# A gated linear attention and spatial-gating MLP on one core: issue order from a list scheduler in the source, grouped attention, a reciprocal for the second scan, and weight low halves on TensorE

## The chip, the cores and the metric

The kernel runs on one core of one Trainium2 chip. The metric is the device time of one execution in microseconds. The engines are TensorE (PE; its weight loads are shown as PEld), VectorE (DVE), ScalarE (ACT), GpSimd (POOL) and SyncE (SP), which here only issues DMAs. Each engine works through its instructions strictly in the order in which they were put into its queue and waits on semaphores for the others.

## The reference

Inputs are q, k, v and alpha of 4 batches, 8 heads, 768 positions and 48 elements a head, and the weights of an MLP (w_in 384 x 1024 and w_out 512 x 384 in float64, w_sg 768 x 768 in float32). First a recurrence over the positions, then the MLP on its result x:

```
state = alpha[:, :, t, :, None] * state + k[:, :, t] (outer) v[:, :, t]
y[:, :, t] = q[:, :, t] . state
x = y with the heads side by side                  # 4 x 768 x 384
h = gelu_tanh(x @ w_in);  u, v = halves of h       # 512 each
v_n = (v - mean) / sqrt(var + 1e-6) * g_ln         # over the 512
v_s = w_sg @ v_n + b_sg                            # over the 768 positions
out = x + (u * v_s) @ w_out
```

## The kernel before

**Attention in chunks.** The 768 positions of a batch are six chunks of 128; with four batches there are 24 chunks, numbered i. Heads lie in pairs: j counts four pairs, e the two heads of a pair, at partitions 0 and 64. For a chunk, `att_load` brings alpha (tile a) and k, q, v (tile kqv, two buffers). `att_prep` makes the running product of alpha from the chunk's start (pf, a scan with a floor) and its counterpart from the end (rf, a second scan backwards that starts from 1/pf at the chunk's end), multiplies q by pf and k by rf, stores pf's last column (pend) and tests alpha's range. `att_scores` multiplies k and q (sc), masks the product on VectorE (at, L176) and transposes k (tp, kn). `att_out` makes y from the state's block matrix s_bd (L211) and from at and v (L214) pair by pair, copies y into xf (two copies and six small DMAs, `pack_x`), and makes the state's update (dl, L223), which VectorE adds and decays (s_c) and ScalarE copies into s_bd.

**Precision.** The MLP's operands are split into a high and a low half of a faster 32-bit type, and each product is three matmuls (`mm3`, L243 to L245): high by high, high by low, low by high. `x_split` makes the halves of x (xh, xl). The weights are split when they come: `split_f32` for w_sg (twelve pieces), `split_f64` for w_in (eight pieces) and w_out (four), which build a float32 from the float64's two words on VectorE (L107, L109, L112, L116, L118) and the low half on GpSimd (L99, L119, L120).

**The MLP** has four products: V (`mlp_v`, one per chunk, 9 matmuls of 512 columns; then gelu, moments, the root on GpSimd, the norm and its halves), U (`mlp_u`, eight a batch, 9 matmuls of 384), P (`mlp_spatial`, mm_s, eight a batch, 18 matmuls; then scale on VectorE, the gate product on GpSimd, high half on ScalarE, low half on VectorE), and R (`mlp_out`, mm_o, six a batch, 12 matmuls; then x is added and the result stored). hf counts the two halves of the positions.

**Order.** The source runs the attention of batch b and, slab by slab between its chunks, P and R of batch b - 1; V and U of a batch follow behind its last chunk (batch 0 has them in between). FILL spreads the weight pieces over batch 0, WARM puts three matmuls without use before each of its y. The program is built with `schedule_with_timeline_sim=True`: a planner then reorders each engine's instructions by simulated times, so that scores and y of a chunk come to lie between single matmuls of the MLP. TensorE starts on twelve matmuls of 128x512 without use (wps).

Of the kernel before, what the change touches and what calls it, by code (L numbers as in the profile page):

```python
# [9 lines left out]
F32 = mybir.dt.float32  # L10
# [11 lines left out]
P = 128  # L22
# [13 lines left out]
WARM = (3, 3, 3, 3, 3, 3)  # L36
FILL = (0, 0, 2, 2, 2, 2, 2, 2, 2, 2, 2, 2, 4)
EPS = 1e-6
F64_MIN_AS_F32 = float(np.array(0x38100000, np.uint32).view(np.float32))


@with_exitstack
def tile_gla_gmlp(ctx: ExitStack, tc: tile.TileContext, aT, kqv, w_in, w_sgT, w_out, g_ln, b_sg, out):
# [4 lines left out]
    late = []  # L48
# [46 lines left out]
    def split_f32(dst_hi, dst_lo, src):  # L95
        raw = stage.tile([P, TH], F32, tag="raw32", name="raw32", bufs=2)
        nc.sync.dma_start(raw, src)
        nc.scalar.copy(dst_hi, raw)
        nc.gpsimd.tensor_tensor(dst_lo, raw, dst_hi.bitcast(F32), op=ALU.subtract)  # L99

    def split_f64(dst_hi, dst_lo, src):
        raw = stage.tile([P, TH, 2], I32, tag="raw64", name="raw64", bufs=3)
        nc.sync.dma_start(raw, src.bitcast(I32).rearrange("p (n two) -> p n two", two=2))
        w0, w1 = raw[:, :, 0], raw[:, :, 1]
        mag = stage.tile([P, TH], F32, tag="mag", name="mag", bufs=2)
        nc.scalar.activation(mag, w1.bitcast(F32), AF.Abs)
        nc.vector.tensor_scalar_max(mag, mag, F64_MIN_AS_F32)  # L107
        top = stage.tile([P, TH], I32, tag="top", name="top", bufs=2)
        nc.vector.tensor_scalar(  # L109
            top, mag.bitcast(I32), 3, 0x3FFFFFF8, op0=ALU.logical_shift_left, op1=ALU.bitwise_and,  # L110
        )
        nc.vector.scalar_tensor_tensor(top, w1, -0x40000000, top, op0=ALU.bitwise_and, op1=ALU.bitwise_or)  # L112
        topf = top.bitcast(F32)
        nc.scalar.copy(dst_hi, topf)
        pw = mag.bitcast(I32)
        nc.vector.tensor_scalar(pw, top, -0x800000, None, op0=ALU.bitwise_and)  # L116
        rest = pw.bitcast(F32)
        nc.vector.scalar_tensor_tensor(rest, w0.bitcast(U32), 2.0 ** -52, rest, op0=ALU.mult, op1=ALU.mult)  # L118
        nc.gpsimd.tensor_tensor(topf, topf, dst_hi.bitcast(F32), op=ALU.subtract)  # L119
        nc.gpsimd.tensor_tensor(dst_lo, topf, rest, op=ALU.add)  # L120

    def w_in_piece(half, j):
        sl = slice(j * TH, (j + 1) * TH)
        hi = wi_hi[:, half].rearrange("p k f -> p (k f)")[:, sl]
        lo = wi_lo[:, half].rearrange("p k f -> p (k f)")[:, sl]
        split_f64(hi, lo, w_in[half, :, sl])

    def w_sg_piece(s, j):
        sl = slice(j * TH, (j + 1) * TH)
        split_f32(ws_hi[:, s, sl], ws_lo[:, s, sl], w_sgT[s * P:(s + 1) * P, sl])  # L130
# [5 lines left out]
    st = {}  # L136

    def att_load(i):
        a = att.tile([P, NP * C1 + 1], F32, tag="a", name="a")
        nc.sync.dma_start(a, aT[i])  # L140
        kqv_t = att.tile([P, 3, NP, C], F32, tag="kqv", name="kqv_t")
        nc.sync.dma_start(kqv_t, kqv[i])
        st[i] = dict(a=a, k=kqv_t[:, 0], q=kqv_t[:, 1], v=kqv_t[:, 2])

    def att_prep(i):
        s = st[i]
        a, k, q = s["a"], s["k"], s["q"]
        n = NP * C1
        pf = att1.tile([P, NP, C1], F32, tag="pf", name="pf")
        nc.vector.tensor_tensor_scan(  # L150
            pf.rearrange("p j t -> p (j t)"), a[:, 0:n], p_flr.rearrange("p j t -> p (j t)"),
            initial=0.0, op0=ALU.mult, op1=ALU.max,
        )
        fl = r_flr[i % 2]
        nc.vector.reciprocal(fl[:, :, C], pf[:, :, C])
        rf = att1.tile([P, NP, C1], F32, tag="rf", name="rf")
        nc.vector.tensor_tensor_scan(  # L157
            rf.rearrange("p j t -> p (j t)")[:, ::-1], a[:, n:0:-1], fl.rearrange("p j t -> p (j t)")[:, ::-1],
            initial=0.0, op0=ALU.mult, op1=ALU.max,
        )  # L160
        nc.gpsimd.tensor_copy(pend[:, i], pf[:, :, C])
        nc.gpsimd.tensor_tensor(k, k, rf[:, :, 1:], op=ALU.mult)  # L162
        nc.vector.tensor_tensor(q, q, pf[:, :, 1:], op=ALU.mult)  # L163
        av = a[:, 0:n].rearrange("p (j t) -> p j t", t=C1)[:, :, 1:]
        nc.scalar.activation(av, av, AF.Relu, bias=alo, scale=-1.0, accum_out=low[:, i:i + 1])  # L165

    def att_scores(i):
        s = st[i]
        k, q = s["k"], s["q"]
        sc = ps.tile([P, 2, NP, C], F32, tag="sc", name="sc")  # L170
        for j in range(NP):
# [3 lines left out]
        at = att1.tile([P, 2, NP, C], F32, tag="at", name="at")  # L175
        nc.vector.tensor_tensor(  # L176
            at.rearrange("p e j t -> p (e j) t"), sc.rearrange("p e j t -> p (e j) t"),
            mask[:, None, :].to_broadcast([P, 2 * NP, C]), op=ALU.mult,
        )
        s["at"] = at  # L180
        if i % NCH < NCH - 1:
            tp = ps.tile([P, NP, P], F32, tag="tp", name="tp")
            for j in range(NP):
                nc.tensor.transpose(tp[:, j], k[:, j], ident)
            kn = att1.tile([P, NP, P], F32, tag="kn", name="kn")
            nc.scalar.copy(kn, tp)
            s["kn"] = kn

    def pack_x(xf, tsl, y):
        y3 = att.tile([P, C], F32, tag="y3", name="y3")  # L190
        nc.scalar.copy(y3, y[:, NP - 1])
        nc.scalar.copy(xf[:, :, tsl], y[:, 0:NK])
        for kk in range(NK):
            for e in range(2):
                nc.sync.dma_start(
                    xf[64 * e + D:64 * e + 64, kk, tsl], y3[64 * e + 16 * kk:64 * e + 16 * kk + 16, :],
                )

    def keep_warm(o, n):
        for _ in range(n):  # L200
            nc.tensor.matmul(o.rearrange("p j t -> p (j t)"), warm[:, :P], warm, start=True, stop=True)

    def att_out(i, xf):
        b, c = divmod(i, NCH)
        s = st[i]
        y = ps.tile([P, NP, C], F32, tag="y", name="y")
        if b == 0:
            keep_warm(y, WARM[c])
        for j in range(NP):
            if c > 0:  # L210
                nc.tensor.matmul(y[:, j], s_bd[:, j], s["q"][:, j], start=True, stop=False)  # L211
            for e in range(2):
                r = slice(64 * e, 64 * e + 64)
                nc.tensor.matmul(y[r, j], s["v"][:, j, r], s["at"][:, e, j], start=(c == 0), stop=True)  # L214
        tsl = slice((c % CPH) * C, (c % CPH + 1) * C)
        pack_x(xf, tsl, y)
        if c < NCH - 1:
            dl = ps.tile([P, NP, D], F32, tag="dl", name="dl")
            kn = s["kn"]
            for j in range(NP):  # L220
                for e in range(2):
                    r = slice(64 * e, 64 * e + 64)
                    nc.tensor.matmul(dl[r, j], kn[:, j, r], s["v"][:, j, 64 * e:64 * e + D], start=True, stop=True)  # L223
            pb = pend[:, i, :, None].to_broadcast([P, NP, D])
            if c > 0:
                nc.vector.tensor_tensor(s_c, s_c, dl, op=ALU.add)
                nc.vector.tensor_tensor(s_c, s_c, pb, op=ALU.mult)
            else:
                nc.vector.tensor_tensor(s_c, dl, pb, op=ALU.mult)
# [289 lines left out]
```

## Time and profile before

| | us |
|---|---|
| median of three runs (lowest, highest) | 445.02 (444.12, 446.96) |
| span of the profiled execution, first to last instruction | 439.6 |
| median less span | 5.4 |
| PE busy, PEld busy | 402.6, 336.9 |
| DVE, ACT, POOL busy | 279.7, 147.0, 174.5 |

The profile is of one execution. "Busy" is the time in which an engine had an instruction in work; matmuls overlap, and their durations run over the next one's start, so the distance from start to start tells the price of one. A row of the timeline gives start, duration, engine, line, operation, tiles and count, and in brackets how long the engine had stood idle and what ended that. A group's row gives the sum of busy time and the mean of one in ns. A row of a stretch gives, after its length, the busy time and count of PE, PEld, DVE, ACT and POOL, the granted TensorE clock (1.00 is full), the DMA engines' share and GB/s.

### The profile page before, as it was taken

The numbers are of one execution on the slowest core, as the hardware profiler recorded it, in microseconds if no ns is written. First come the engines' busy times: TensorE is split into PE (matmuls) and PEld (weight loads), VectorE is DVE, ScalarE is ACT, GpSimd is POOL, SyncE is SP. The second block draws the span as 40 slices with busy tenths as digits, with TensorE's granted clock in tenths as the row PEclk, the third lists the DMA queues.
The fourth block names the chain that finished last, engine by engine and source line by source line (L and its number), as shares of the span: only waits on it lengthen the run. The fifth ranks groups of instructions, "written<-read, shape, count | busy, mean of one in ns | idle before, by whom it ended". The sixth has DMA issues, their size and how long they took to land.

```text
span 439.6 us, 7271 instructions
## 1 busy us (share of the span) xinstructions
PE 402.6 (92%) x2724; PEld 336.9 (77%) x2728; DVE 279.7 (64%) x410; ACT 147.0 (33%) x330; POOL 174.5 (40%) x200
## 2 busy tenths in 40 slices
PE   6489586978899999999999999999999999999994
PEld 2356375657788878788988887788988887899993
DVE  8999999999544676565454656665465732732331
ACT  2533553643332332254232331353222321541010
POOL 3756687787240432423230632423232530412030
PEclk9959788999999999999999999999999999999999
DMA  8744643451024332302024332202123201000101
GB/s 309 240 136 137 207 148 97 156 171 29 26 78 136 118 102 60 122 5 74 24 78 137 119 102 93 88 5 73 26 76 131 78 5 38 22 2 0 53 2 60
DMA packets 18762, 39.15 MB, mean 89 GB/s; under 512 B 4000, under 2 KB 10912, under 8 KB 18720
## 3 DMA queue, kind: packets, MB, share of 16 engines
q1 hardware_dynamic: 18720, 38.61, 26.8%
q8 instruction: 23, 0.38, 0.3%
q14 instruction: 19, 0.16, 0.1%
HBM read 32.70 MB, written 4.72 MB: 85 GB/s over the span
## 4 chain that ended last, share of the span: by engine, by line
PE 56%; DVE 16%; DMA 7%; issue 2%; ACT 1%; SPq 1%; POOL 1%; DVEq 0%; POOLq 0%
DMA kqv_t<-in_kqv 6%; PE mm_s L243 6%; PE mm_s L245 5%; PE mm_s L244 5%; DVE pf L150 4%; PE y L214 4%; PE y L211 4%; PE mm_u L243 3%; PE mm_v L243 3%; PE sc L174 3%; PE mm_o L244 3%; PE mm_v L244 3%; PE mm_u L245 3%; PE mm_u L244 3%; PE mm_v L245 3%; PE mm_o L243 3%
## 5 line engine op out<-in xcount | busy, mean ns | idle before, releaser
L283 POOL TENSOR_TENSOR g<-g,u 128x384 f32<-128x384 f32 x32 | 32.4, 1014 | 100.3 <-DVE g L282 100.2
L243 PE MATMUL mm_s<-ws_hi,vh 128*128 128x384 f32 x192 | 67.6, 352 | 0.0
L245 PE MATMUL mm_s<-ws_hi,vl 128*128 128x384 f32 x192 | 64.8, 339 | 2.2 <-DVE vl L265 2.2
L244 PE MATMUL mm_s<-ws_lo,vh 128*128 128x384 f32 x192 | 64.8, 338 | 0.0
L162 POOL TENSOR_TENSOR kqv_t<-kqv_t,rf 128x512 f32<-128x512 f32 x24 | 36.9, 1537 | 63.0 <-DMA kqv_t<-in_kqv 56.1
L214 PE MATMUL y<-at,kqv_t 128*64 128x128 f32 x384 | 42.9, 307 | 12.2 <-DVE at L176 12.0
L211 PE MATMUL y<-kqv_t,s_bd 128*128 128x128 f32 x160 | 39.0, 328 | 3.5 <-ACT s_bd L232 2.7
L150 DVE TENSOR_TENSOR_SCAN pf<-a,p_flr 128x516 f32<-128x516 f32 x24 | 41.1, 1713 | 1.3 <-DMA a<-in_aT 0.7
L284 ACT CAST gh<-g 128x384 fp32r<-128x384 f32 x32 | 16.5, 514 | 74.1 <-POOL g L283 74.1
L285 DVE TENSOR_TENSOR gl<-g,gh 128x384 fp32r<-128x384 f32 x32 | 19.2, 600 | 32.8 <-ACT gh L284 32.7
L214 PEld LDWEIGHTS y<-at,kqv_t 128*64 128x64 f32 x384 | 21.1, 142 | 23.7 <-DVE at L176 14.4
L211 PEld LDWEIGHTS y<-kqv_t,s_bd 128*128 128x128 f32 x160 | 26.9, 200 | 15.6 <-issue 10.6
L282 DVE SCALAR_TENSOR_TENSOR g<-mm_s,g_col,b_bc 128x384 f32<-128x384 f32 x32 | 19.6, 613 | 29.7 <-PE mm_s L245 29.7
L165 ACT ACTIVATE a<-a,alo 128x512 f32<-128x512 f32 x24 | 17.4, 723 | 62.9 <-DVE rf L157 62.8
L245 PEld LDWEIGHTS mm_s<-ws_hi,vl 128*128 128x128 f32 x192 | 36.1, 188 | 2.5 <-DVE vl L265 2.5
L243 PEld LDWEIGHTS mm_s<-ws_hi,vh 128*128 128x128 f32 x192 | 36.1, 188 | 1.2 <-DVE r L292 0.3
L243 PE MATMUL mm_u<-xh,wi_hi 128*128 128x384 f32 x96 | 35.1, 369 | 2.1 <-ACT vg L253 2.1
L163 DVE TENSOR_TENSOR kqv_t<-kqv_t,pf 128x512 f32<-128x512 f32 x24 | 18.9, 789 | 27.4 <-DMA kqv_t<-in_kqv 27.4
L244 PEld LDWEIGHTS mm_s<-ws_lo,vh 128*128 128x128 f32 x192 | 36.2, 188 | 0.0
L174 PEld LDWEIGHTS sc<-kqv_t 64*128 64x128 f32 x384 | 26.6, 191 | 10.7 <-issue 9.4
L174 PE MATMUL sc<-kqv_t 64*128 64x128 f32 x384 | 34.3, 295 | 0.0
L244 PE MATMUL mm_o<-gl,wo_hi 128*128 128x384 f32 x96 | 33.6, 350 | 0.5 <-DVE gl L285 0.2
(86 smaller groups left out, 870.1 us busy)
## 6 DMA issues: line engine op xcount, KB each, us to landing
kqv_t<-in_kqv SPq DMA_DIRECT2D x24, 768.0 KB, 4.3
a<-in_aT SPq DMA_DIRECT2D x24, 258.5 KB, 2.7
out_x<-r SPq DMA_DIRECT2D x24, 192.0 KB, 2.3
raw<-in_w_in SPq DMA_DIRECT2D x8, 384.0 KB, 4.1
raw<-in_w_sgT SPq DMA_DIRECT2D x12, 192.0 KB, 3.2
xf<-y SPq DMA_DIRECT2D x144, 8.0 KB, 2.6
raw<-in_w_out SPq DMA_DIRECT2D x4, 384.0 KB, 3.2
b_bc<-in_b_sg SPq DMA_DIRECT2D x1, 384.0 KB, 7.7
```

The lines of the kernel that those rows point to most:

```text
L150: nc.vector.tensor_tensor_scan(pf.rearrange("p j t -> p (j t)"), a[:, 0:n], p_flr.rearrange("p j t -> p (j t)"), initial=0.0, op0=ALU.mult ...
L162: nc.gpsimd.tensor_tensor(k, k, rf[:, :, 1:], op=ALU.mult)
L163: nc.vector.tensor_tensor(q, q, pf[:, :, 1:], op=ALU.mult)
L174: nc.tensor.matmul(sc[:, e, j], k[r, j], q[r, j], start=True, stop=True)
L211: nc.tensor.matmul(y[:, j], s_bd[:, j], s["q"][:, j], start=True, stop=False)
L214: nc.tensor.matmul(y[r, j], s["v"][:, j, r], s["at"][:, e, j], start=(c == 0), stop=True)
L243: nc.tensor.matmul(o, lh, rh, start=(idx == 0), stop=False)
L244: nc.tensor.matmul(o, lh, rl, start=False, stop=False)
L245: nc.tensor.matmul(o, ll, rh, start=False, stop=(idx == n - 1))
L282: nc.vector.scalar_tensor_tensor(g, o, g_col[:, d:d + 1], b_bc[:, tsl], op0=ALU.mult, op1=ALU.add)
L283: nc.gpsimd.tensor_tensor(g, g, u, op=ALU.mult)
L285: nc.vector.tensor_tensor(gl[:, d], g, gh[:, d].bitcast(F32), op=ALU.subtract)
```

## The change

- Every piece of work becomes a step with an engine, a cost in ns, the steps it follows and the buffers it takes. `Plan.issue` walks through them once, in Python, and emits each step's instructions in the order of a list scheduler: of the steps that could start soonest on an engine, the one that is due first. A list of TensorE's products, `units`, written by hand, gives the dues. The built-in planner is off inside (`manual_schedule`). Some steps (k, x low, gate, the low halves not on TensorE) go to GpSimd or VectorE, the norm to VectorE or ScalarE, whichever would end first by the plan.
- Attention comes in groups: the outputs of chunk i - 1 (O) and the scores of chunk i (S) one behind the other, with whole products of the MLP between the groups.
- The second scan, its floor r_flr and the small reciprocal go. After q is multiplied by pf, pf is inverted in place (128x512) and k multiplied by it. kqv has three buffers.
- The state stays in s_c; its block matrix s_bd and the copies into it go. The state's product is eight 64x64 matmuls ahead of all of at and v, not one 128x128 for each pair between them.
- The low halves of w_in and of w_sg's first half are made on TensorE (identity times the value less identity times the high half, in PSUM) and copied by ScalarE. w_sg's first half comes in two loads through the tiles gh and gl. w_out and w_sg's second half get their place from the plan. The raw tiles share one ring of two.
- WARM and FILL go; the first warm-up matmuls are 128x128. mask and p_flr become bf16.

The core of the diff:

```
+    REACH = {"pe": 215, "act": 40, "dve": 40, "pool": 75, "sp": 0}
...
+    def issue(self, units, ahead):
...
+            for e, c in ready.items():
+                t0 = min(x[0] for x in c)
+                t, way_order, n, way = min((x for x in c if x[0] <= t0 + (150 if e == "pe" else 60)), key=lambda x: x[1])
+                if best is None or (t, way_order) < best[:2]:
+                    best = (t, way_order, n, way)
...
-        nc.vector.reciprocal(fl[:, :, C], pf[:, :, C])
-        rf = att1.tile([P, NP, C1], F32, tag="rf", name="rf")
-        nc.vector.tensor_tensor_scan(
-            rf.rearrange("p j t -> p (j t)")[:, ::-1], a[:, n:0:-1], fl.rearrange("p j t -> p (j t)")[:, ::-1],
...
+    def invert(i):
+        pf = st[i]["pf"][:, :, 1:]
+        nc.vector.reciprocal(pf, pf)
...
-            if c > 0:
-                nc.tensor.matmul(y[:, j], s_bd[:, j], s["q"][:, j], start=True, stop=False)
...
+        if c > 0:
             for j in range(NP):
                 for e in range(2):
                     r = slice(64 * e, 64 * e + 64)
+                    nc.tensor.matmul(
+                        y[r, j], s_c[r, j], s["q"][r, j], start=(j == 0), stop=False, skip_group_check=True,
+                    )
...
+        def low_pe():
+            t["o"] = o = psm.tile([P, TH], F32, tag="mm", name="mm_w")
+            nc.tensor.matmul(o, ident, t["top"].bitcast(F32), start=True, stop=False)
+            nc.tensor.matmul(o, nident, dst_hi, start=False, stop=False)
+            nc.tensor.matmul(o, ident, t["mag"], start=False, stop=True)
...
+        plan.add(("recip", i), "dve", 670, lambda i=i: invert(i), [("q", i), ("pend", i)])
+        plan.add(
+            ("k", i), "pool", 1250, lambda i=i: scale_k(i, nc.gpsimd), [("recip", i), ("kqv", i)],
+            other=("dve*", 670, lambda i=i: scale_k(i, nc.vector)),
+        )
...
+    def group(i):
+        r = [(("O", i - 1), 2400)]
+        if i < n:
+            r.append((("S", i), 1500))
+        return r
...
+        for d in range(ND):
+            units.append((("P", b, 0, d), 3120))
+            if d > 0:
+                units.append((("U", b, 1, d), 1560))
+        if b < B - 1:
+            units += group(g + 2)
+            units += [(("R", b, 0, kk), 2080) for kk in range(NK)] + [(("P", b, 1, 0), 3120)]
+            units += group(g + 3)
+            units += [(("P", b, 1, d), 3120) for d in (1, 2, 3)]
+            units += group(g + 4)
...
+    keep_warm(ps.tile([P, NP, C], F32, tag="y", name="wps"), NWARM)
+    with tc.manual_schedule():
+        plan.issue([name for name, _ in units], 4)
```

By `units`, batch 0 runs O and S of its six chunks with V0 to V3 strewn in, then U of its first half, V4, V5, the scores of chunk 6 and one U, the group of O6 and S7, and then its first P. In later batches V3, the four U of the first half, V4, V5, one U and a group stand ahead of the first P.

More of the change, by code (lines that the diff above doesn't have):

```diff
@@ L42, in tile_gla_gmlp, with run @@
+def run(steps):
+    for s in steps:
+        (s[0] if isinstance(s[0], tuple) else s)[2]()
 @with_exitstack
@@ L47, in tile_gla_gmlp @@
     mlp = ctx.enter_context(tc.tile_pool(name="mlp", bufs=1))
-    late = []
     dram = ctx.enter_context(tc.tile_pool(name="dram", bufs=1, space=bass.MemoryType.DRAM))
@@ new lines, in split_f32, with load, high, low_half @@
+    def split_f32(dst_hi, dst_lo, src, raw=None):
+        t = dict(raw=raw)
+        def load():
+            raw = stage.tile([P, TH, 2], I32, tag="raw", name="raw", bufs=2)
+            t["raw"] = raw.bitcast(F32).rearrange("p n two -> p (n two)")[:, 0:TH]
+            nc.sync.dma_start(t["raw"], src)
+        def high():
+            nc.scalar.copy(dst_hi, t["raw"])
+        def low_half(eng):
+            eng.tensor_tensor(dst_lo, t["raw"], dst_hi.bitcast(F32), op=ALU.subtract)
+        def low_pe():
+            t["o"] = o = psm.tile([P, TH], F32, tag="mm", name="mm_w")
+            nc.tensor.matmul(o, ident, t["raw"], start=True, stop=False)
+            nc.tensor.matmul(o, nident, dst_hi, start=False, stop=True)
+        def low_act():
+            nc.scalar.copy(dst_lo, t["o"])
+        return dict(load=load, high=high, low_half=low_half, low_pe=low_pe, low_act=low_act, parts=t)
@@ L222, in att_out @@
                     r = slice(64 * e, 64 * e + 64)
[L223 to L229, printed above, removed]
+                    nc.tensor.matmul(
+                        y[r, j], s_c[r, j], s["q"][r, j], start=(j == 0), stop=False, skip_group_check=True,
+                    )
@@ L277, in mlp_spatial @@
+    def mlp_spatial(vn, u, g, hf, d):
         sl = slice(d * P, (d + 1) * P)
         tsl = slice(hf * TH, (hf + 1) * TH)
-        o = psm.tile([P, TH], F32, tag="mm", name="mm_s")
-        mm3(o, [(vn[s][0][:, sl], vn[s][1][:, sl], ws_hi[:, s, tsl], ws_lo[:, s, tsl]) for s in range(NS)])
-        g = late[0].tile([P, TH], F32, tag="g", name="g", bufs=2)
-        nc.vector.scalar_tensor_tensor(g, o, g_col[:, d:d + 1], b_bc[:, tsl], op0=ALU.mult, op1=ALU.add)
-        nc.gpsimd.tensor_tensor(g, g, u, op=ALU.mult)
@@ L284, in mlp_spatial @@
[L284 to L294 removed]
+        t = {}
@@ new lines, in product, with scale, gate @@
+        def product():
+            t["o"] = psm.tile([P, TH], F32, tag="mm", name="mm_s")
+            mm3(t["o"], [(v["vh"][:, sl], v["vl"][:, sl], ws_hi[:, s, tsl], ws_lo[:, s, tsl]) for s, v in enumerate(vn)])
+        def scale():
+            t["g"] = mlp.tile([P, TH], F32, tag="g", name="g", bufs=2)
+            nc.vector.scalar_tensor_tensor(
+                t["g"], t["o"], g_col[:, d:d + 1], b_bc[:, tsl], op0=ALU.mult, op1=ALU.add,
+            )
+        def gate(eng):
+            eng.tensor_tensor(t["g"], t["g"], u["u"], op=ALU.mult)
@@ new lines, in high, with low_half @@
+        def high():
+            if d == 0:
+                g["h"] = mlp.tile([P, ND, TH], F32R, tag="gh", name="gh")
+            nc.scalar.copy(g["h"][:, d], t["g"])
+        def low_half():
+            if d == 0:
+                g["l"] = mlp.tile([P, ND, TH], F32R, tag="gl", name="gl")
+            nc.vector.tensor_tensor(g["l"][:, d], t["g"], g["h"][:, d].bitcast(F32), op=ALU.subtract)
+        return [
+            ("pe", 3120, product), ("dve", 585, scale),
+            (("pool", 1000, lambda: gate(nc.gpsimd)), ("dve*", 545, lambda: gate(nc.vector))), ("act", 510, high),
+            ("dve*", 545, low_half),
+        ]
@@ new lines, in count @@
+    def count():
+        check["cnt"] = cnt = ps.tile([1, 1], F32, tag="dl", name="cnt")
+        nc.tensor.matmul(cnt, okp, ones, start=True, stop=True)
+    end = due[("R", B - 1, 0, 0)]
+    plan.add(("ok",), "dve", 600, in_range, [("range", n - 1), ("pend", n - 1)], due=end)
+    plan.add(("cnt",), "pe", 100, count, [("ok",)], takes=[("dl", 1, [("cnt_i",)])], due=end + 3000)
+    plan.add(("cnt_i",), "dve", 150, lambda: nc.vector.tensor_copy(cnt_i, check["cnt"]), [("cnt",)], due=end + 6000)
```

752 lines of the change are left out of this document (518 added, 234 removed).

## Prediction

> **What bounds the kernel now.** I read the busy totals and the tenths first, then the span cut where its character changes, then each engine's instructions in order of time.
>
> ```profile
> PE 402.6 (92%) x2724; PEld 336.9 (77%) x2728; DVE 279.7 (64%) x410; ACT 147.0 (33%) x330; POOL 174.5 (40%) x200
> DVE  8999999999544676565454656665465732732331
> ...
> 0.00:106.40 106.40, 80.40 (x548) 56.85 (x552) 102.85 (x139) 48.05 (x111) 73.03 (x82) 0.89 0.50 166
> 106.40:433.00 326.60, 322.13 (x2178) 280.08 (x2176) 176.01 (x271) 98.95 (x220) 101.46 (x119) 1.00 0.20 64
> 433.00:439.60 6.60, 0.05 (x1) 0.00 (x0) 0.88 (x2) 0.00 (x0) 0.00 (x0) 0.88 0.29 97
> ...
> 20.00:40.00 20.00, 15.52 (x102) 9.92 (x103) 19.97 (x25) 7.26 (x18) 14.62 (x13) 0.74 0.43 135
> ```
>
> Two kernels run one after the other. Up to 106.4 us, where the first mm_s product starts, VectorE is busy 102.85 us: it sets the pace, and the DMA engines are half idle. From 106.4 to 433.0 TensorE is busy 322.13 of 326.60 and VectorE only 176. Then comes a tail of 6.6. The 92% of the first line is a mean over both. So work taken from VectorE counts only in the first stretch, work taken from TensorE only in the second. The span is 439.6; the median of the three runs is 445.02, so 5.4 us lie around it, which I carry over.
>
> What fills VectorE up to 111 us, group by group (busy sum, mean):
>
> ```profile
> L150 DVE TENSOR_TENSOR_SCAN pf<-a,p_flr 128x516 f32<-128x516 f32 x10 | 14.5, 1447 | 0.8 <-DMA a<-in_aT 0.7
> L118 DVE SCALAR_TENSOR_TENSOR mag<-raw,mag 128x384 f32<-128x384 uint32 x12 | 14.3, 1195 | 0.0
> L157 DVE TENSOR_TENSOR_SCAN rf<-a,r_flr 128x516 f32<-128x516 f32 x10 | 13.7, 1375 | 0.2
> L112 DVE SCALAR_TENSOR_TENSOR top<-raw,top 128x384 int32<-128x384 int32 x12 | 11.4, 952 | 0.1
> L107 DVE TENSOR_SCALAR mag<-mag 128x384 f32<-128x384 f32 x12 | 9.1, 755 | 0.8 <-ACT mag L106 0.7
> L109 DVE TENSOR_SCALAR top<-mag 128x384 int32<-128x384 int32 x12 | 6.2, 521 | 0.1
> L116 DVE TENSOR_SCALAR mag<-top 128x384 int32<-128x384 int32 x12 | 4.8, 402 | 0.1
> ...
> 28.49 0.53 DVE L112 SCALAR_TENSOR_TENSOR top<-raw,top 128x384 int32<-128x384 int32 x1
> ...
> 29.05 0.36 DVE L116 TENSOR_SCALAR mag<-top 128x384 int32<-128x384 int32 x1
> 29.33 0.35 DVE L107 TENSOR_SCALAR mag<-mag 128x384 f32<-128x384 f32 x1
> ...
> L118 DVE SCALAR_TENSOR_TENSOR mag<-raw,mag x12: 559/1291/1373, 15.7 to 97.5; 128x384 f32<-128x384 uint32 x12
> ```
>
> The five steps of the twelve float64 pieces sum to 45.8 us, 3.8 a piece. The single rows show what they take undisturbed: 0.53, 0.36, 0.35, and 0.56 as L118's shortest, some 2.1 a piece with L109 like L107. The rest goes while GpSimd runs its own products beside them (73 us busy in this stretch).
>
> **The change, part by part.**
>
> *Second scan to reciprocal.* Ten second scans in the stretch, 13.7 us, go; a reciprocal of 128x512 comes, which the trace has only with four elements.
>
> ```profile
> L155 DVE RECIPROCAL r_flr<-pf x24: 157/169/183, 4.9 to 340.5; 128x4 f32<-128x4 f32 x24
> ...
> L438 DVE TENSOR_REDUCE ok_range<-pend 128x1 f32<-128x96 f32 x1 | 0.3, 253 | 0.0
> ...
> L437 DVE TENSOR_REDUCE ok_range<-low 128x1 f32<-128x24 f32 x1 | 0.2, 177 | 0.1
> ```
>
> Two reduces give 76 ns for 72 elements, so 1.06 ns an element over 152 ns. Four elements at that pace make 156, and 186 at eight times it; the reciprocal shows 157 to 183, median 169, nearer the first. Bounds: 0.69 and 4.5 us; I take 0.69. The Trainium skill (VectorE: DVE Perf Modes, "First, the fixed hardware budget") says that reciprocal is an iterative divide with a repeat count of 8; read as eight passes an element it speaks against this edit, at 4.5. No run here shows a long one; it is a rival below.
>
> *Weights.* The four w_out pieces go behind the first spatial products: 4 x 3.8 = 15.3 us leave the first stretch. The low halves of the eight w_in pieces go from GpSimd to TensorE and ScalarE, so their VectorE steps should run near 2.1 instead of 3.8: 13.6 us. VectorE's first stretch becomes 102.85 - 13.7 - 15.3 - 13.6 + 8 x 0.69 = 66; two chunks fewer are prepared ahead (two scans, 2.9): 63, and less if the other operations are disturbed less. It runs from about 3.6 on, so its work ends near 67; were GpSimd to disturb the pieces as now, near 80. The loads move too: w_sg's first halves come as two transfers instead of six, the raw ring shrinks from three and two buffers to two; the DMA share is 0.50 now, and the same bytes or fewer are wanted before the first P, so I cost that at nothing, hidden behind the work of VectorE and TensorE; uncovered it is the landing of one transfer at a time. ScalarE gets fourteen low halves and loses the copies into the state's block matrix; with 48 us busy of 106 it hides either, and the state comes to the next y without that copy. Steps for which either GpSimd or VectorE is picked (k, x low, gate) change sides at like cost, since the one disturbs the other; I count them as they are now.
>
> *TensorE's own prices,* as start-to-start distances:
>
> ```profile
> 8.07 1.16 PE L174 MATMUL sc<-kqv_t 64*128 64x128 f32 x16
> ...
> 139.00 1.16 PE L174 MATMUL sc<-kqv_t 64*128 64x128 f32 x16
> 140.10 0.66 PE L184 MATMUL tp<-ident,kqv_t 128*128 128x128 f32 x4
> 140.51 0.42 PE L243 MATMUL mm_s<-ws_hi,vh 128*128 128x384 f32 x1
> ...
> 146.24 0.44 PE L214 MATMUL y<-at,kqv_t 128*64 128x128 f32 x4
> 146.61 0.49 PE L211 MATMUL y<-kqv_t,s_bd 128*128 128x128 f32 x2
> 147.03 0.44 PE L214 MATMUL y<-at,kqv_t 128*64 128x128 f32 x4
> 147.30 0.62 PE L223 MATMUL dl<-kqv_t,kn 128*64 128x48 f32 x14
> 147.85 0.44 PE L243 MATMUL mm_s<-ws_hi,vh 128*128 128x384 f32 x1
> ...
> 166.29 0.38 PE L211 MATMUL y<-kqv_t,s_bd 128*128 128x128 f32 x2
> 166.43 0.42 PE L243 MATMUL mm_o<-gh,wo_hi 128*128 128x384 f32 x1
> ...
> 189.63 1.09 PE L214 MATMUL y<-at,kqv_t 128*64 128x128 f32 x16
> 190.65 0.49 PE L174 MATMUL sc<-kqv_t 64*128 64x128 f32 x2
> ...
> 386.26 0.40 PE L243 MATMUL mm_v<-wi_hi,xh 128*128 128x512 f32 x1
> 388.36 0.34 PE L243 MATMUL mm_u<-xh,wi_hi 128*128 128x384 f32 x1
> ...
> 394.72 0.34 PE L243 MATMUL mm_s<-ws_hi,vh 128*128 128x384 f32 x1
> 397.90 0.34 PE L243 MATMUL mm_s<-ws_hi,vh 128*128 128x384 f32 x1
> ```
>
> V (9 matmuls) is 2.10, P (18) is 3.18, so U (9) is 1.59 and R (12) 2.12; 63.4 a batch. Scores 1.10, transposes 0.41, dl 0.63 (14 in 0.55). A y with state is four times L211 and L214, 0.42 + 0.37: 3.16. But sixteen L214 in one go take 1.02, so 2.14 belongs to the state product and to changing shape eight times. Afterwards the state product is sixteen 64x64 instructions in one block. Bounds: the same pace as L214 (1.02) and no two beside each other (16 x 0.107 = 1.7, from the pair's 0.21 below). I take 1.05, nearest in shape: a y costs 2.07, **1.09 less in each of 20 chunks**.
>
> A low half on TensorE is two or one float32 products of 384 columns and a short one. The L211 pair inside the mm_o stream costs 0.14 and a slow step behind it, about 0.21 for 128 columns: 0.64 for 384 (bounds 0.4, three times L214's pace, and 1.26, three times 0.42). A w_in piece is 2 x 0.64 + 0.17 = 1.45, a w_sg piece 0.81: 16.5 in all, every bit in the first stretch.
>
> *TensorE's first stretch afterwards.* Seven scores 7.7, six transposes 2.5, six y 6.1 + 5 x 1.05, five dl 3.2, V 12.6, U of one half 6.4, low halves 16.5, changes of shape 1.3: 61.5. From 8.1 (first scores; the reciprocal path scan, q, reciprocal, k is no longer than now) that is **69.6 at the least**, a little behind VectorE. Both feed each other: scores, mask and outputs of a chunk follow one another, and the six mask products of 1.2 us have only weights and V to cover them. I add 8.4 and take **78** for the start of the first P (70 to 92).
>
> *The second stretch.* Now it holds, by the counts of its rows, P and R of batch 0 (38.1), three batches (190.2), 14.75 y with state (46.6), 2.25 without (2.3), 16.5 scores (18.2), 14 transposes (5.7), 14 dl (8.8): 309.9. The other 16.7 of 326.6 are 4.5 idle and 12.2 of changing shape, since scores and y are strewn in between the MLP's matmuls. Afterwards: 38.1 + 190.2, four U left over (6.4), 18 y 18.4 and their 15 state products 15.8, 15 dl 9.5, 17 scores 18.7, 14 transposes 5.7: 302.7. O and S come as a group, so I leave 8 for idling and shape (3 to 20): **311**.
>
> *Waits that are added.* An S stands right behind O; what waits on it in TensorE's queue is all the MLP work behind, and for that ScalarE and VectorE. A third kqv buffer starts its load two groups ahead, which covers the k product. VectorE and GpSimd have 150 us of room each in 311. V5's matmuls wait for six pack transfers on SP's queue, x high and low; V3, four U and V4 (10.5 us) cover that.
>
> *Tail.* R's products are no longer mixed by depth, so the last R waits at its tenth matmul for the last gate:
>
> ```profile
> 426.83 0.62 DVE L282 SCALAR_TENSOR_TENSOR g<-mm_s,g_col,b_bc 128x384 f32<-128x384 f32 x1 [0.27 <-PE mm_s L245]
> ...
> 429.19 0.56 DVE L285 TENSOR_TENSOR gl<-g,gh 128x384 fp32r<-128x384 f32 x1 [1.74 <-ACT gh L284]
> ```
>
> From scale to low half 2.9, and 0.3 before; nine matmuls cover 1.6: 1.6 more (0 to 3).
>
> **Sum:** 78 + 311 + 6.6 + 1.6 = 397; with 5.4 around it **402 us**. Against now: first stretch -28, second -16, tail +1.6.
>
> **Rivals.**
> *A slow start.* Eighteen keep-warm matmuls go and the first twelve shrink to a quarter.
>
> ```profile
> 22.97 0.69 PE L214 MATMUL y<-at,kqv_t 128*64 128x128 f32 x4 [4.48 <-DVE at L176]
> ```
>
> After this wait four L214 take 0.62 where they take 0.37 elsewhere, and the granted clock of 20 to 40 us is 0.74. At 0.74 throughout, 61.5 become 83: P starts at 91, with the same mask waits partly inside, so 415, to 425 if they are not. For it: the waits are where the recurrence is serial. Against: 61 us of work in 70 leave fewer long gaps than 80 busy in 106. The Trainium skill (TensorE: Matmul & The Clock Gate, "HAM oscillation — how this bites in real kernels") says that a gap beyond about 3.4 us halves the clock; by that rule, too, gaps and not sums decide, and the 4.48 above agrees.
> *A long reciprocal.* At 4.5 us VectorE gets 8 x 3.8 = 30 more in the first stretch: P at 100 to 108, and 425 to 433 in all, more with the later 16. The four-element row speaks against it.
> *Groups that stall, slower than now.* The order is fixed by constants; the second stretch's scans run beside GpSimd. If k comes late at each group, TensorE stands still, and nothing of the MLP may pass. There are 18 groups; 43 us are to be lost, so it decides from 2.4 us a group and is slower by 1% from 2.7: 450 to 460 at 3. Against: 4.5 us idle in all of that stretch now.
> *The list order is no better than the planner's.* Then the weights disturb as before: VectorE's first stretch is 102.85 - 13.7 + 5.5 and its start of 3.6, so 98, and the second stretch keeps all 16.7 of idling and shape, 319: 98 + 319 + 8.2 + 5.4 = 431, and up to 445 where w_out's work, no longer early, is late instead. For it: both orders are made from costs, not from the chip. Against: what costs most, w_out's steps and the low halves, is moved by the dependences and the engine, not by the order.
>
> **Chances.** Forecast (387 to 412) 0.68; slow start (412 to 428) 0.15; long reciprocal 0.05; stalled groups 0.07; no better order 0.05. Range **387 to 428**, leaving out most of the last three, 0.17. Three runs tell about 1% from no change. Slower is the stalled groups, 0.07; within 1% I put 0.04, the upper ends of the long reciprocal and of no better order; faster 0.89.
>
> **What would show it.** P's first matmul near 78 and VectorE near 0.9 busy before; reciprocals of 0.69; the pieces' last VectorE step (rest) near 0.56; sixteen 64x64 instructions in about 1.05; second stretch near 311 with TensorE at 0.97; granted clock near 0.9 at the start; the last R waiting about 1.6 us once. Wrong: a first P past 92, or waits of TensorE on k or q summing to over 10 us.

## The result, and the profile after

The changed kernel takes **430.2 us** (426.3 to 431.1), the kernel before in the same runs 444.6: a ratio of 0.966, with an interval from 0.960 to 0.973. It is faster, by 14 us and not by the 43 of the forecast; 402 was said, and 430 lies 2 us past the upper end of the range. Medians and ratios, here and below, leave out a few executions in a slower state, two of them of 1.2 and 2.1 ms.

First the busy totals and VectorE's tenths of the kernel after, then its span cut at the first P and at the last product (stretch, busy time and count of PE, PEld, DVE, ACT and POOL, granted clock, DMA share, GB/s).

```profile
PE 385.2 (90%) x2928; PEld 342.3 (80%) x2928; DVE 321.1 (75%) x466; ACT 145.2 (34%) x337; POOL 39.3 (9%) x87
...
DVE  6889999798996799797948778975848675353341
```
```profile
0.00:110.26 110.26, 80.44 (x613) 61.91 (x614) 98.82 (x144) 51.60 (x123) 11.64 (x31) 0.88 0.45 155
110.26:422.60 312.34, 304.77 (x2318) 280.39 (x2316) 221.91 (x323) 93.57 (x215) 27.62 (x56) 0.99 0.21 70
422.60:428.30 5.70, 0.00 (x0) 0.00 (x0) 0.39 (x1) 0.00 (x0) 0.00 (x0) 0.74 0.13 43
```

The first P starts at 110.3, 3.9 later than before, where 78 was forecast. Ahead of it VectorE is busy for 98.8 us (102.9 of 106.4 before), where 63 was forecast. The second stretch is 312.3 (326.6 before, 311 forecast). The profile of the kernel before is one of its shortest executions (a span of 439.6, where its other runs reach 446.2), so differences of a few us to its stretches are not exact. And work has changed sides: VectorE went from 279.7 to 321.1 in all, GpSimd from 174.5 to 39.3. VectorE's groups show what it is busy with:

```profile
L337 DVE RECIPROCAL pf<-pf 128x512 f32<-128x512 f32 x24 | 80.3, 3344 | 2.0 <-ACT pend L329 1.4 <-ACT u L520 0.5
L323 DVE TENSOR_TENSOR_SCAN pf<-a,p_flr 128x516 f32<-128x516 f32 x24 | 29.4, 1224 | 2.0 <-DMA a<-in_aT 1.9
...
L540 DVE TENSOR_TENSOR g<-g,u 128x384 f32<-128x384 f32 x32 | 17.8, 556 | 0.8
...
L341 DVE TENSOR_TENSOR kqv_t<-kqv_t,pf 128x512 f32<-128x512 f32 x23 | 15.7, 681 | 0.2
...
L439 DVE TENSOR_TENSOR xl<-xf,xh 128x384 fp32r<-128x384 f32 x23 | 12.3, 536 | 7.9 <-ACT xh L435 7.9
```

The reciprocal takes **3.34 us**, not 0.69. That is 80.3 us in all, 63.7 more than forecast and more than twice what the scan that it replaced takes (1.38 before, by L157). The last three rows are steps for which the plan may pick an engine: all 32 gate products, 23 of 24 k and 23 of 24 x low went to VectorE, on which the reciprocal already lies.

### The profile page after: what moved, and what is told of

Read it like the earlier page. It is cut to its first block, busy times and chain, and to the rows that moved or that the text cites. A ratio compares the mean times of both kernels' runs of the same rounds, so it can differ in the third digit from the quotient of the medians.

```text
span 428.3 us, 7480 instructions
## 1 busy us (share of the span) xinstructions
PE 385.2 (90%) x2928; PEld 342.3 (80%) x2928; DVE 321.1 (75%) x466; ACT 145.2 (34%) x337; POOL 39.3 (9%) x87
## 4 chain that ended last, share of the span: by engine, by line
PE 62%; DVE 17%; issue 6%; DMA 4%; ACT 4%; SPq 3%; POOL 2%; DVEq 0%; ACTq 0%
DVE pf L337 7%; PE mm_s L456 7%; PE mm_s L458 7%; PE mm_s L457 7%; PE sc L354 5%; PE y L391 4%; PE mm_o L456 3%; PE mm_o L457 3%; PE mm_o L458 3%; PE y L385 3%; SPq L427 3%; PE mm_u L456 2%; DMA xf<-y 2%; PE mm_u L457 2%; PE mm_u L458 2%
## 5 line engine op out<-in xcount | busy, mean ns | idle before, releaser
L337 DVE RECIPROCAL pf<-pf 128x512 f32<-128x512 f32 x24 | 80.3, 3344 | 2.0 <-ACT pend L329 1.4
L456 PE MATMUL mm_v<-wi_hi,xh 128*128 128x512 f32 x72 | 31.0, 430 | 7.7 <-ACT vg L471 6.4
L458 PE MATMUL mm_v<-wi_hi,xl 128*128 128x512 f32 x72 | 30.1, 419 | 5.6 <-DVE xl L439 5.6
L456 PE MATMUL mm_o<-gh,wo_hi 128*128 128x384 f32 x96 | 33.2, 346 | 0.3 <-ACT gh L545 0.3
L457 PE MATMUL mm_u<-xl,wi_hi 128*128 128x384 f32 x96 | 33.0, 343 | 0.0
L458 PE MATMUL mm_u<-xh,wi_lo 128*128 128x384 f32 x96 | 32.9, 343 | 0.0
L391 PE MATMUL y<-at,kqv_t 128*64 128x128 f32 x384 | 28.3, 293 | 5.1 <-DVE at L363 5.1
L458 PE MATMUL mm_o<-gh,wo_lo 128*128 128x384 f32 x96 | 32.3, 337 | 0.0
L483 POOL TENSOR_SCALAR rstd<-mv 128x1 f32<-128x1 f32 x24 | 7.6, 317 | 266.5 <-DVE mv L479 266.4
L363 DVE TENSOR_TENSOR at<-sc,mask 128x1024 f32<-128x1024 f32 x24 | 29.0, 1210 | 2.5 <-PE sc L354 2.3
```

The source lines that it names most:

```text
L337: nc.vector.reciprocal(pf, pf)
L363: nc.vector.tensor_tensor(at.rearrange("p e j t -> p (e j) t"), s["sc"].rearrange("p e j t -> p (e j) t"), mask[:, None, :].to_broadcast([ ...
L456: nc.tensor.matmul(o, lh, rh, start=(idx == 0), stop=False)
L457: nc.tensor.matmul(o, lh, rl, start=False, stop=False)
L458: nc.tensor.matmul(o, ll, rh, start=False, stop=(idx == n - 1))
L483: nc.gpsimd.tensor_scalar(rstd, t["mv"][:, 1:2], EPS, None, op0=ALU.add)
```

## The experiments

The theories: **(A)** the reciprocal's own price; **(B)** that the plan, which carries 670 ns for it, gives VectorE steps that it has no time for; **(C)** that the weights were not taken out of the first stretch; **(D)** that the order, the state's product or the low halves do not bring what was counted; **(E)** the slow clock at the start. A summary (first P and second stretch from one profiled execution each), the kernel before of the same runs standing at 443.4 to 444.9:

| kernel | us, median | ratio to before (interval) | first P | second stretch |
|---|---|---|---|---|
| after | 430.2 | 0.966 (0.960 to 0.973) | 110.3 | 312.3 |
| recip_cost | 414.0 | 0.931 (0.925 to 0.937) | 102.2 | 304.5 |
| short | 396.3 | 0.893 (0.889 to 0.896) | 88.7 | 302.3 |
| scan | 402.3 | 0.906 (0.901 to 0.911) | 93.4 | 301.6 |
| wo_later | 430.1 | 0.968 (0.960 to 0.975) | 107.3 | 317.7 |
| b_state | 441.1 | 0.990 (0.985 to 0.995) | 110.9 | 323.6 |
| b_recip | 446.5 | 1.004 (0.999 to 1.008) | 119.1 | 318.9 |
| scan_planner | 415.7 | 0.936 (0.928 to 0.944) | 97.8 | 310.2 |
| scan_norm | 401.3 | 0.901 (0.895 to 0.908) | 91.7 | 302.3 |
| scan_low | 406.7 | 0.912 (0.905 to 0.919) | 97.0 | 301.0 |
| scan_warm | 403.2 | 0.904 (0.897 to 0.911) | 94.5 | 301.5 |

**recip_cost**: the same instructions, only the plan's cost put right.

```
-        plan.add(("recip", i), "dve", 670, ...
+        plan.add(("recip", i), "dve", 3340, ...
```

> Only the plan's cost of the 128x512 reciprocal is set to what it takes on the chip (3340 ns in place of 670); the work is the same, the order and the choice of engines may change. Theory A (the reciprocal's own time in VectorE's queue, nine of them ahead of the first P, 24 us more than forecast): VectorE has the same work, so 424 to 432 us, first P at 105 or later. Theory B (a plan that is wrong by 2.7 us at 24 places puts steps on the wrong engine and in front of the wrong wait): most of the lost 32 us come back, 400 to 412, with more work on GpSimd than the 39 us of the changed kernel.

```profile
0.00:102.20 102.20, 77.17 (x613) 60.78 (x614) 92.50 (x134) 52.27 (x122) 16.84 (x34) 0.90 0.50 163
102.20:406.70 304.50, 302.20 (x2318) 278.13 (x2316) 217.93 (x314) 95.76 (x218) 44.21 (x72) 1.00 0.23 73
```
```profile
L337 DVE RECIPROCAL pf<-pf 128x512 f32<-128x512 f32 x24 | 80.3, 3345 | 0.5
```
```profile
L439 POOL TENSOR_TENSOR xl<-xf,xh 128x384 fp32r<-128x384 f32 x13 | 13.6, 1045 | 99.7 <-ACT xh L435 99.7
...
L341 POOL TENSOR_TENSOR kqv_t<-kqv_t,pf 128x512 f32<-128x512 f32 x4 | 5.0, 1247 | 52.8 <-DVE pf L337 52.8
```

One number in the source brings 16 us: the first P comes 8.1 earlier, the second stretch is 7.8 shorter. The reciprocals cost the same 80.3; thirteen x low and four k now run on GpSimd, and the steps lie in another order. 414.0 lies between the two ranges, 10 below A's and 2 above B's: B holds, for about half of what is missing. Which of the two, the sides or the order, does it was not taken apart.

**short**: a product of the reciprocal's shape in its place.

```
-        nc.vector.reciprocal(pf, pf)
+        nc.vector.tensor_tensor(pf, pf, pf, op=ALU.mult)
```

> The reciprocal is replaced by a product of pf with itself, which writes the same tile at the price that the prediction gave the reciprocal (0.69 us); k is scaled by the wrong numbers. Order and everything else as in the changed kernel. Theory A: nine times 2.65 = 24 us go from VectorE ahead of the first P, which starts at 80 to 87; 402 to 407 us. Theory C (TensorE's lower granted clock at the start, 0.76 to 0.84 from 40 to 100 us, is what holds the first P): the clock stays low and the first P stays past 95; 415 or more.

```profile
0.00:88.70 88.70, 72.86 (x614) 57.23 (x614) 74.97 (x144) 51.66 (x123) 12.57 (x31) 0.96 0.56 192
88.70:391.00 302.30, 301.30 (x2318) 278.52 (x2315) 185.32 (x323) 95.85 (x215) 26.81 (x56) 1.00 0.23 72
```

The product takes 0.68, so this is the kernel with the price that the forecast gave the reciprocal; what it leaves out is the right scale of k. It takes 396.3, less than the 402 to 407 expected. The forecast's sum comes near it, 402 less the 3.6 us by which it overrated what lies around the span (below), but that is luck in part: the first P is 10.7 later than forecast, the second stretch 8.7 and the tail 2.4 shorter. Between 430.2 and 396.3 only this one instruction differs: 33.8 us, of which 16.2 go when the plan knows the price (recip_cost) and 17.7 when the work itself goes; by the profiled spans 31.5, 15.9 and 15.6. A and B together settle what separates the two kernels.

**scan**: the backward scan put back, beside all other parts; a GpSimd step clears pf after q, and the small reciprocal seeds the scan; alpha's tile gets one column more, and the range test waits for the scan.

```
-        pf = st[i]["pf"][:, :, 1:]
-        nc.vector.reciprocal(pf, pf)
+        nc.vector.reciprocal(pf[:, :, C], pf[:, :, C])
+        pr = pf.rearrange("p j t -> p (j t)")[:, ::-1]
+        nc.vector.tensor_tensor_scan(pr, a[:, n:0:-1], pr, initial=0.0, op0=ALU.mult, op1=ALU.max)
+    def clear(i):
+        nc.gpsimd.memset(st[i]["pf"][:, :, 0:C], 0.0)
...
-        plan.add(("recip", i), "dve", 670, ...
+        plan.add(("recip", i), "dve*", 1395, ...
```

> The changed kernel with the backward scan in place of the reciprocal: GpSimd clears pf, VectorE inverts its last column (128x4) and scans backwards into pf, planned at 1395 ns. The output is the reference's. Theory A: 9 x (3.34 - 1.40) = 17.5 us less ahead of the first P: 410 to 415. Theory B: the plan fits the chip, so more comes back: 398 to 408.

```profile
L339 DVE TENSOR_TENSOR_SCAN pf<-a,pf 128x516 f32<-128x516 f32 x24 | 29.6, 1233 | 2.8 <-POOL pf L342 0.6
...
L337 DVE RECIPROCAL pf<-pf 128x4 f32<-128x4 f32 x24 | 4.1, 172 | 0.4 <-ACT pend L329 0.3
```

The scan and its seed take 1.4 us a chunk, the reciprocal 3.34. The version that does the whole computation and leaves this one part of the change out takes 402.3, 28 us less than the change as made and inside B's range.

**wo_later**: the loads of w_out also wait for the first P.

```
+            at("load"), "sp", 330, p["load"], [("P", 0, 0, 0)] if name[0] == "wo" else [],
```

> The loads of w_out are made to wait for the first P; otherwise the changed kernel. In its trace all twelve float64 pieces go through VectorE ahead of the first P, so w_out is not prepared later at all. Theory A (VectorE's queue sets the first P): four pieces of 2.1 and two or three of their low halves at 1.1 leave, first P at 100 to 103, 420 to 424 us, if w_out then comes in time for the first R; where it does not, 428 to 436. If VectorE's queue is not what counts: 430.

Nothing is gained, where A expected 420 to 424: the first P comes 3.0 earlier and the second stretch is 5.4 longer. VectorE's work ahead of the first P falls only from 98.8 to 92.1, since the plan puts five low halves of w_sg (2.8 us) into the place, and the scores of one chunk moved behind the first P too. What left the first stretch came back in the second. C falls as a cause in this kernel, although the observation behind it is right (below).

**b_state** and **b_recip**: one part each in the kernel before, under its own planner. b_state takes s_bd out and puts eight 64x64 matmuls (sixteen instructions in the profile) ahead of all of at and v; b_recip puts one reciprocal of 128x512 in place of the second scan.

```
-                nc.tensor.matmul(y[:, j], s_bd[:, j], s["q"][:, j], start=True, stop=False)
+                    nc.tensor.matmul(y[r, j], s_c[r, j], s["q"][r, j], start=(j == 0), stop=False, ...)
```
```
-        nc.vector.tensor_tensor_scan(rf...[:, ::-1], a[:, n:0:-1], fl...[:, ::-1], ...)
+        nc.vector.reciprocal(rf[:, :, 1:], pf[:, :, 1:])
```

> The kernel before with the state's product alone changed: eight 64x64 matmuls from s_c ahead of the eight of at and v, no block matrix and no copies into it; the planner still sets the order. By the prediction's price (a y with state 3.16 to 2.07) 14.75 such y in the second stretch give 16 us: 426 to 430, if the planner keeps the sixteen together. If the shape changes come back because the planner strews them, 434 to 442. A theory in which the changed kernel's second stretch gained from the groups alone: 440 or more.

> The kernel before with the reciprocal alone: 128x512 in place of the second scan and the small reciprocal. Theory A (VectorE sets the first stretch): ten reciprocals of 3.34 for ten scans of 1.38 and 0.17 are 18 us more ahead of the first P: 455 to 465. If a longer VectorE step is hidden there: 445. The prediction's price (0.69) would have made it 436.

Neither gave what the price alone promised: b_state gains 1% (441.1, where 426 to 430 was expected), and b_recip, at 446.5, lies near the 445 of a step that is hidden, not at A's 455 to 465. Of b_state the stretches and what TensorE waits for longest (total, times, longest):

```profile
0.00:110.90 110.90, 85.09 (x606) 63.14 (x606) 106.48 (x145) 47.41 (x104) 79.84 (x85) 0.80 0.50 162
110.90:434.50 323.60, 312.83 (x2284) 277.33 (x2282) 174.26 (x266) 85.11 (x186) 100.12 (x115) 0.99 0.20 64
```
```profile
PE mm_o L247 <- ACT gh L288: 6.6, 3, 2.7
PE mm_v L247 <- ACT xh L241: 6.2, 3, 5.4
```

TensorE's work in the second stretch fell by 9.3 (322.1 to 312.8), where the price made it 16, and its length by only 3.0: its idle time grew from 4.5 to 10.8, and the first row, three waits of R for the gate's high half, is part of that. The second row is a wait ahead of the first P, which comes 4.5 later. So some of the gain per y is there and turned into waits, in an order that the planner made anew; which waits that order had to have was not tested. b_recip has the same 3.34 us a reciprocal:

```profile
0.00:119.10 119.10, 92.96 (x618) 65.08 (x618) 113.32 (x129) 53.90 (x120) 67.90 (x81) 0.84 0.49 160
119.10:438.00 318.90, 316.65 (x2112) 276.35 (x2112) 201.99 (x257) 94.27 (x211) 102.93 (x120) 1.00 0.19 61
```
```profile
L155 DVE RECIPROCAL rf<-pf 128x512 f32<-128x512 f32 x24 | 80.2, 3340 | 0.4
```

Its first P comes 12.7 later, as A says, but 66 more of TensorE's instructions lie after P in before than here (2178 against 2112), and the second stretch is 7.7 shorter: a planner that puts other products into the time that VectorE needs hides most of the price. The same edit costs 1.6 us here, not told apart from nothing; in the list order it is 12 with its true cost in the plan (recip_cost against scan) and 28 with the wrong one.

**scan_planner**: the kernel scan, with the built-in planner left on over it.

```
-    with tc.manual_schedule():
+    if True:
```

> The kernel with the backward scan, but with the built-in planner on: it may reorder what the list scheduler emitted, on every engine. Theory D (the order from the list and the groups are worth the 8 us of fewer shape changes and the packed start): 410 to 425, with attention strewn between the MLP's matmuls again. If the dependences and the moved work are what counts and not the order: within 4 us of 402.

The list order is worth 13.5 us, 8.6 of them in the second stretch (310.2 against 301.6). So the forecast's rival "no better order" is out, and D with it for the order.

**scan_norm**: in scan, the norm of v never goes to ScalarE.

```
-("act", 760, norm_act)
+None
```

> The kernel with the backward scan, with the norm of v always on VectorE (the plan put some on ScalarE, where it waits for GpSimd's root and holds up all that follows: one 5.6 us wait of V on the gelu ahead of it, after which the granted clock falls to 0.80). If that wait is a head-of-line one on ScalarE: 5 to 8 us less, 394 to 398, with the first P near 86. If VectorE only takes over the delay: 400 to 404.

In after, short, scan and others TensorE stands for about 6 us once before a V, waiting for ScalarE's vg, and a norm on ScalarE waits there for GpSimd (2.1 us in scan). Without that norm the wait is still there, and the time is that of VectorE taking over the delay, 400 to 404:

```profile
70.63 0.80 PE L461 MATMUL mm_v<-wi_hi,xh 128*128 128x512 f32 x1 [5.45 <-ACT vg L476]
```
```profile
65.61 0.51 ACT L440 CAST xh<-xf 128x384 fp32r<-128x384 f32 x1 [3.52 <-DMA xf<-y]
...
67.81 1.14 ACT L504 CAST vh<-vg 128x512 fp32r<-128x512 f32 x2 [0.97 <-DVE vg L500]
69.40 0.20 ACT L329 COPY pend<-pf 128x4 f32<-128x4 f32 x1 [0.46 <-DVE pf L323]
69.98 0.60 ACT L476 ACTIVATE vg<-mm_v 128x512 f32<-128x512 f32 x1 [0.38 <-DVE vl L508]
```

Other things stand in ScalarE's queue ahead of the vg in question: x high, which waits 3.5 us for the transfers of y, then vh, pend. The norm as the one cause is refuted; the 1.0 us between the two medians is less than these runs can tell. That the whole queue is the cause is what the rows suggest, and no run took it away.

**scan_low** and **scan_warm**: in scan, the low halves made on GpSimd or VectorE; twelve bf16 matmuls without use ahead of each of batch 0's six y.

```
-        on_pe = name[0] in ("wv", "wu")
+        on_pe = False
-    SGPE = 1
+    SGPE = 0
```
```
+        if i < NCH:
+            for _ in range(12):
+                nc.tensor.matmul(y..., warm, warm, start=True, stop=True)
```

> The kernel with the backward scan put back (402.27, first P at 93.4), and in it the low halves of the eight w_in and six w_sg pieces taken off TensorE again and made on GpSimd or VectorE, as the plan picks. TensorE loses 8 x 3 + 6 x 2 = 36 matmuls of 384 columns, some 15 us of its 76 busy before the first P. Theory A (the prediction: low halves beside VectorE's steps disturb these and make them 3.8 instead of 2.1 us a piece): VectorE, 80 busy of 93.4 with the low halves away, gets 10 to 14 more, first P 100 to 106, time 409 to 415. Theory B (TensorE's own work and its half clock set the first P): first P 3 to 8 earlier, time 394 to 399. Neither: within 2 of 402, the two cancelling.

> The same kernel with the backward scan, and twelve bf16 matmuls of 128x128 without use ahead of each of the six y of batch 0, in y's own bank. Theory A (slow start: the granted clock of 0.80 from 60 to 93.4 costs that much): the clock rises to 0.95 or more there, the 27 us of TensorE's work in that stretch shrink by some 4 and the first P comes 3 to 4 earlier, time near 398. Theory B (waits set the pace, the low clock is only the trace of a wait that is there anyway): first P stays within 1.5 of 93.4, time 401 to 404.

First VectorE's groups in scan_low up to the first P (the two low-half steps and, between them, a piece's last step), then the stretch from 60 us to the first P of scan and of scan_warm, and the V wait in scan_warm:

```profile
L275 DVE TENSOR_TENSOR top<-top,wi_hi 128x384 f32<-128x384 f32 x8 | 4.2, 552 | 0.2
L260 DVE SCALAR_TENSOR_TENSOR mag<-raw,mag 128x384 f32<-128x384 uint32 x8 | 4.2, 550 | 0.0
L278 DVE TENSOR_TENSOR wi_lo<-top,mag 128x384 fp32r<-128x384 f32 x8 | 4.1, 548 | 0.0
```
```profile
60.00:93.40 33.40, 27.18 (x153) 21.11 (x152) 28.05 (x59) 18.53 (x42) 13.41 (x21) 0.80 0.28 87
```
```profile
60.00:94.50 34.50, 25.27 (x159) 20.04 (x155) 29.45 (x62) 20.33 (x45) 12.80 (x21) 0.90 0.31 96
```
```profile
72.79 0.79 PE L464 MATMUL mm_v<-wi_hi,xh 128*128 128x512 f32 x1 [6.92 <-ACT vg L479]
```

Low halves on TensorE bring 3.5 to 4.4 us (against scan_warm of the same runs, against scan), a third of the 13.6 that the forecast took off VectorE for them; 406.7 lies between its theories. Taken off TensorE, those of w_in run on VectorE, 8.3 us of it, and the pieces' last step stays at 0.55, where the kernel before has 1.19: with GpSimd little used (39 to 61 us in these kernels, 174.5 before) the pieces keep their short steps. What the low halves would cost on GpSimd beside them no run here shows. In scan_warm the granted clock rises from 0.80 to 0.90 and the first P does not come earlier; the V waits 6.92 instead of 5.64. E falls for this kernel: taking half of the slow clock away moved nothing ahead. And in short, where only the reciprocal is gone, the clock ahead of the first P is 0.96 against 0.88 in after.

## Why the prediction was wrong, and where it was right

**The step that failed is the reciprocal's price.** The bounds, 0.69 and 4.5, held 3.34; the value taken inside them did not. The row used to choose, four elements in 157/169/183 ns, cannot tell. By an estimate, 3344 less the 152 of the forecast over 512 elements is 6.2 ns each, and four of these give 152 + 25 = 177, well inside that row's spread, while the 156 of the short end lies just below its least. "Nearer the first" was read out of a median 13 ns from one end and 17 from the other, less than the row's own spread of 26. The Trainium skill (VectorE: DVE Perf Modes, "First, the fixed hardware budget") gives reciprocal as an iterative divide with a repeat count of 8. The trace has 5.9 times the 1.06 ns of the reduces' slope, so the direction is right, and eight full passes an element are too many. The rival "a long reciprocal" gave P at 100 to 108 and 425 to 433 in all; 110 and 430 came, though by another sum than its own: it counted the work alone at 4.5 us each, and about half of what came is the plan's. It had a chance of 0.05.

**A price that stands twice.** The forecast rated a long reciprocal only as VectorE's time. But the source carries the same wrong figure as a plan's cost, and recip_cost shows that this half weighs as much: 16 of 34 us. The step "k, x low and gate change sides at like cost" failed with it: 78 of 80 such products fell to the engine that the reciprocals already filled. By themselves they did little harm: in short the same 78 lie on VectorE, and it takes 396.3.

**VectorE's first stretch**, 63 forecast, 98.8 found. Of VectorE in the kernel after, up to the first P:

```profile
L337 DVE RECIPROCAL pf<-pf 128x512 f32<-128x512 f32 x9 | 30.1, 3345 | 1.5 <-ACT pend L329 1.4
...
L251 DVE SCALAR_TENSOR_TENSOR top<-raw,top 128x384 int32<-128x384 int32 x12 | 6.8, 583 | 0.0
...
L341 DVE TENSOR_TENSOR kqv_t<-kqv_t,pf 128x512 f32<-128x512 f32 x8 | 5.5, 686 | 0.2
L260 DVE SCALAR_TENSOR_TENSOR mag<-raw,mag 128x384 f32<-128x384 uint32 x10 | 5.2, 547 | 0.1
L241 DVE TENSOR_SCALAR mag<-mag 128x384 f32<-128x384 f32 x12 | 4.1, 346 | 1.7 <-ACT mag L238 1.7
L245 DVE TENSOR_SCALAR top<-mag 128x384 int32<-128x384 int32 x12 | 4.0, 348 | 0.0
...
L257 DVE TENSOR_SCALAR mag<-top 128x384 int32<-128x384 int32 x11 | 3.7, 347 | 0.1
L439 DVE TENSOR_TENSOR xl<-xf,xh 128x384 fp32r<-128x384 f32 x5 | 2.9, 579 | 0.0
L275 DVE TENSOR_TENSOR top<-top,wo_hi 128x384 f32<-128x384 f32 x3 | 1.7, 554 | 0.2 <-ACT wo_hi L254 0.2
...
L278 DVE TENSOR_TENSOR wo_lo<-top,mag 128x384 fp32r<-128x384 f32 x2 | 1.0, 550 | 0.0
```

Nine reciprocals of 3.34 instead of eight of 0.69 are 24.6 more, k and x low 8.4, and ten forward scans where eight were forecast 2.4. And w_out did not leave: twelve pieces start here, not eight. Four times L241, L245 and L251, three times L257, twice L260 and the two low-half rows are 9.9 us. "The four w_out pieces go behind the first spatial products" was taken from where the source lists them; the plan lets a step go as soon as its engine and buffers are free. These sum to 108, 10 above the measured time, since other operations take less than before: V's norm and low half 5.6 us (L495, L503) instead of 12.0 (L261, L265), a part of the norms being on ScalarE, and a scan 1.22 instead of 1.45. One reading of the forecast was off as well: its 13.7 us of second scans were counted up to 111 us, while the stretch up to 106.4 holds nine, 12.5 us. The pieces' own forecast was right: 0.35, 0.35, 0.58, 0.35 and 0.55 make 2.2 a piece (2.1 said).

**TensorE's first stretch.** Apart from the reciprocal the 78 were too early too; short has 88.7. One term was miscounted, as the rows of the kernel after up to the first P show:

```profile
L354 PE MATMUL sc<-kqv_t 64*128 64x128 f32 x128 | 11.1, 322 | 13.2 <-DVE kqv_t L341 7.1 <-issue 5.6 <-PE mm_w L268 0.4
L391 PE MATMUL y<-at,kqv_t 128*64 128x128 f32 x112 | 9.7, 327 | 5.1 <-DVE at L363 5.1
...
L456 PE MATMUL mm_u<-xh,wi_hi 128*128 128x384 f32 x15 | 5.2, 349 | 1.1 <-ACT vg L471 1.1
```

At 16 a chunk these are eight scores and seven y, and at three a slab five U, not seven, six and four: the group of O6 and S7 and one more U lie ahead of the first P, 1.1 + 0.4 + 1.0 + 0.6 + 1.6 = 4.7 us by the forecast's prices, moved from the second stretch to the first at no change in the sum. The other 6 us are as long as the one V wait of 6.1 in short; that this wait is what they are is argued, no run took it away:

```profile
PE mm_v L456 <- ACT vg L471: 6.1, 1, 6.1
PE sc L354 <- DVE kqv_t L341: 5.0, 1, 5.0
```

The second row is the first scores' wait, of which most was forecast: in short they start at 8.34, where 8.1 was said; in after the reciprocal makes that wait 7.1 and the start 10.48.

**The second stretch** hit 311 with 312.3 by two errors that cancel. Its bare sum of 302.7 is met by short (302.3) and scan (301.6), so groups with whole products between them cost next to no idle time, and the 8 added for it weren't needed. In after the reciprocal filled their place: TensorE is idle for 7.6 us there, against 1.0 in short, and works 3.5 us longer at a clock of 0.99. Two of its waits (total, times, longest):

```profile
PE mm_v L456 <- ACT vg L471: 6.4, 1, 6.4
PE mm_v L458 <- DVE xl L439: 5.6, 2, 3.0
```

The first is the V wait of the first stretch. The second lies in the second stretch: two V of later batches that stood for x low, which the plan had put on VectorE. Stalled groups, the rival on the slow side, did not come: TensorE is idle for 7.6 us in the whole stretch (312.34 less 304.77), 0.4 for each of 18 groups even if all were theirs, and the rival decided from 2.4.

**TensorE's prices** were near:

```profile
57.37 1.09 PE L385 MATMUL y<-kqv_t,s_c 64*64 64x128 f32 x16
58.39 1.09 PE L391 MATMUL y<-at,kqv_t 128*64 128x128 f32 x16
59.32 0.62 PE L399 MATMUL dl<-kqv_t,kn 128*64 128x48 f32 x16
...
63.26 0.91 PE L266 MATMUL mm_w<-top,ident 128*128 128x384 f32 x2
...
64.83 0.81 PE L266 MATMUL mm_w<-top,ident 128*128 128x384 f32 x2
```

The state's product takes 1.02 (1.05 said), a y with state 1.95 (2.07), a low half of w_in 1.57 (1.45). **The tail** is 5.7: the last gate runs on VectorE at once behind its scale, and R waits 0.4, not 1.6. **Around the span** lie 1.75 us (430.05 less 428.3), here and in runs of the kernel before (442.29 with a span of 440.5); the 5.4 came from holding one execution's span against a median of others.

## What to carry to other kernels

Where two prices of an operation are far apart and its only row has four elements, whose spread is as wide as the difference looked for, that row chooses neither: both ends need a real chance, and the range has to reach to what the long one costs. A plan with costs in the source is as good as its costs: one wrong number cost as much through the order and the choice of engines as through the instruction itself, so each cost is worth holding against a row of the trace. And what a change takes off one engine is read from where the plan puts it, not from where the source lists it.

## What the runs showed that was not expected

A float32 reciprocal of 128x512 on VectorE takes 3.34 us (means of 3344, 3345 and 3340 ns in after, recip_cost and b_recip, beside an idle GpSimd and a busy one alike), while a product of that shape takes 0.68 and a scan of 516 elements 1.23: the scan takes 2.7 times less than the reciprocal that seemed to save it. The kernel scan, 402.3 (scan_norm 401.3, not told apart), beats both kernels here: 28 us below the change, 41 below the kernel before.
